# Attention and a mixture of experts on one core: weight differences for quarter products made earlier, and quarter products from group 1 on

## The chip, the cores and the metric

The kernel runs on one core of a Trainium2 chip. The time is device time in microseconds (us) of one execution. Three runs of the kernel before took 1044.04, 1045.3 and 1048.0 us; the median is 1045.3. The engines are TensorE (PE, with its weight loads PEld), VectorE (DVE), ScalarE (ACT) and GpSimd (POOL). SyncE (SP) issues DMAs, and so do POOL and ACT.

## The reference

Two steps. The first is attention for 8 batches and 8 heads of width 64: 32 global and 512 local tokens, where local tokens see the global ones and a band of 32 to each side. Its output is 4352 rows of 512 values, x, in batches of 544. The second is a mixture of 8 experts in which every row goes through every expert, weighted by a matrix P that eight normalisations over rows and columns make from the gate's logits:

```python
    logits = x @ w_gate
    logits = logits - logits.max()
    P = np.exp(logits)
    for _ in range(8):
        P /= P.sum(1, keepdims=True) + 1e-09
        P /= P.sum(0, keepdims=True) + 1e-09
        P *= N / E
    out = np.zeros((N, D), dtype=np.float32)
    for e in range(E):
        h = np.maximum(x @ w1[e], 0.0)
        ye = h @ w2[e]
        out += P[:, e:e + 1] * ye
```

Here D is 512, the hidden width F is 1024, E is 8, and the expert weights are w1 (512 x 1024) and w2 (1024 x 512).

## The kernel before

**Two parts.** The order of all instructions is written out by hand. The first part is a software pipeline over 32 slots, four to a batch; slot s works on a pair of heads of batch s // 4. It transposes q and k (`st_A`), makes scores (`st_B`), normalises them (`st_N`), transposes them (`st_D1`, `st_D2`) and multiplies by the values (`st_E`). Every second slot from 9 on carries a step for global queries (`st_G0`, `st_G1`), which ends in the slot after (`st_GN`, `st_G2`, `st_G3`). Between these steps, `f1` puts first-layer products of experts 0 to 3 on PE: relu(x w1), since P is positive and can be multiplied in later. `p_l1` makes eight of them, with ACT or DVE doing the relu (L471, L473), into a tile hT of 1 MB, and stores it to DRAM (hd). The first part's times repeat every 41.07 us, which is four slots.

**Buffers and queues of the first part.** The pool `hpool` has four buffers of 1 MB, tag hT. SP issues, in the order of the code, the loads of q and k (L122, four of 512 KB at the end of each slot 4b), the stores of hT and x, and moves of values. A queue waits in order: an instruction that waits holds all behind it. POOL casts q and k to fp16 (L131), issues the loads of values, and in slots 13, 17, 21 and 25 the conversion of w1 of experts 4 to 7 from fp32 to an fp16 copy in DRAM, w1d (L484).

**The second part** runs over units (m, e): group m is 512 rows (0 to 7, and a half group 8), and e runs in the order 4, 0, 5, 1, 6, 2, 7, 3. Units with an even number (experts 4 to 7) make the first layer here, from x scaled by P; those with an odd number (experts 0 to 3) load h from hd and scale it. The second layer is done for all units by seven half-size products in place of eight (`product`, L928), from sums and differences that DVE makes. While a pair of units has its second layer, the next even unit's first layer is made between those products, in one of two forms:

- the full form, `l1` (L818): 32 matmuls of 512 columns, weights from a tile w1s of 1 MB;
- the quarter form, class `Fast` (L836): seven products of quarter size for each half p of the hidden width, 56 matmuls of 256 columns in all. It needs weights w1q with four raw quarters and three sums and differences (7 x 2 x 256 values a partition, 896 KB for each half), differences of x on DVE (`sums_x`), and copies and additions of partial sums on ACT and DVE (L852, L854, L861, L868).

`WX = {6: 2, 7: 2}` says from which group an expert takes the quarter form: experts 6 and 7, from group 2 on, groups 0 to 7 being whole. `wseq` is the order in which weights go through two buffers (tag w1e); `load_w1` issues the loads on SP when a buffer's last user is done.

**The differences of the weights** are made in group 1. `wseq` holds, after each of the group's full units, an entry ("raw", p): four loads of 128 KB from w1d (L726), four DVE instructions in `prep_w1`, and a store of the 896 KB to w1c on POOL's queue (L741). From group 2 on, w1c is loaded with one DMA for each half (L729).

Of the kernel before, what the change touches and what calls it, by code (L numbers as in the profile page):

```python
# [9 lines left out]
FP16 = mybir.dt.float16  # L10
FP32 = mybir.dt.float32
AF = mybir.ActivationFunctionType
ALU = mybir.AluOpType
# [10 lines left out]
def kernel(  # L24
# [13 lines left out]
    nc = tc.nc  # L38
# [3 lines left out]
    D, E = moe_w_gate.shape  # L42
    F = moe_w1.shape[2]
    P = 128
# [6 lines left out]
    HP = H // 2  # L51
# [17 lines left out]
    hpool = ctx.enter_context(tc.tile_pool(name="hpool", bufs=4))  # L69
# [3 lines left out]
    NL = E // 2  # L73
    hd = [[ydram.tile([P, FT, n], FP16, name=f"hd{e}_{m}") for m, (_, n) in enumerate(groups)] for e in range(NL)]
    xd = [ydram.tile([P, DP, n], FP16, name=f"xd{m}") for m, (_, n) in enumerate(groups)]
    w1d = [ydram.tile([P, DP, F], FP16, name=f"w1d{e}") for e in range(NL, E)]
    pd = ydram.tile([E, NTOK], FP32, name="pd")
    WX = {6: 2, 7: 2}
    w1c = {e: [ydram.tile([P, 7, 2, 256], FP16, name=f"w1c{e}_{p}") for p in range(2)] for e in WX}
    psx = ExitStack()  # L80
    xpool = psx.enter_context(tc.tile_pool(name="xpool", bufs=1, side="right"))
# [10 lines left out]
    with tc.tile_pool(name="att_c", bufs=1) as att_c, \  # L92
# [121 lines left out]
        def run(steps):  # L214
            for f in steps:
                f()
# [6 lines left out]
        f0 = [att_in.tile([P, 4, NJ, Dh], FP32, tag="f32", name="f32", bufs=4) for t in range(2)]  # L223
        for i in range(2):
            for f, src, eng in zip(f0, (q_l, k_l), (nc.scalar, nc.sync)):
                eng.dma_start(out=f[:, 2 * i : 2 * i + 2].rearrange("p h s d -> p h (s d)"),
                              in_=src[0, 2 * i : 2 * i + 2].rearrange("h (p s) d -> p h (s d)", s=NJ))
# [9 lines left out]
        for a in range(2):  # L237
            r = slice(HB * a, HB * (a + 1))
# [15 lines left out]
        for so in range(NJ):  # L254
            for c0, n in ((W, P), (W + Sl, W // NJ)):
                nc.vector.tensor_copy(out=zsel[:, so, c0 : c0 + NJ * n].rearrange("p (x s) -> p x s", s=NJ)[:, :, so],
                                      in_=identity[:, 0:n])
# [143 lines left out]
        def st_G1(b, g):  # L401
            n0 = HP * b + 2 * g
            qg = qgbd[(2 * b + g) % 2]
            gc = slice(Sg * b, Sg * (b + 1))
            sg = ps_po.tile([P, 2 * 512], FP32, tag="po")
            for c0, c1, k0 in ((0, Sl - W, 2 * W), (Sl - W, Sl, W), (Sl, S, None)):
                for pr in range(2):
                    rhs = kgT[:, 2 * g + pr, gc] if k0 is None else kTe[(n0 + pr) % NK][:, k0 : k0 + c1 - c0]
                    nc.tensor.matmul(sg[:, c0:c1], qg[:, pr, :], rhs, start=(pr == 0), stop=(pr == 1))
            m2 = att_wk.tile([P, 4], FP32, tag="m2")  # L410
            nc.vector.reduce_max(out=m2[:, 0:1], in_=sg[:, 0:S], axis=AX.X)  # L411
            nc.vector.tensor_scalar(out=m2[:, 1:2], in0=m2[:, 0:1], scalar1=-scale, scalar2=None, op0=ALU.mult)
            Pg = att_wk.tile([P, S], FP16, tag="Pg")
            nc.scalar.activation(out=Pg, in_=sg[:, 0:S], func=AF.Exp, scale=scale, bias=m2[:, 1:2],
                                 accum_out=m2[:, 2:3])
            gs[(b, g)] = (Pg, m2)
# [60 lines left out]
        def load_w1e(e):  # L477
# [2 lines left out]
            wts[e] = pool.tile([P, DP, F], FP16, name="w1e", **kw)  # L480
            nc.gpsimd.dma_start(out=wts[e], in_=moe_w1[e].rearrange("(dko dki) f -> dki dko f", dki=P))

        def load_w1d(e):
            nc.gpsimd.dma_start(out=w1d[e - NL], in_=moe_w1[e].rearrange("(dko dki) f -> dki dko f", dki=P))  # L484

        fill = [(k % NL, k // NL) for k in range(NL * (B + 1))]
        n1 = 0
# [100 lines left out]
        for s in range(HP, NU + 1):  # L588
            slot = s
            b, hp = divmod(s, HP)  # L590
            g1 = s in gat
            g23 = s - 1 in gat
            if g1:
                gn = divmod(gat[s], 2)
            if g23:
                gp = divmod(gat[s - 1], 2)
            if s == HP:
                st_A(s + 1)
                st_B(s, 2)
                st_E(s - 1)  # L600
                st_N(s, 0, 6)
                st_N(s, 6, NHB)
                select_v(1, 0, (0, 1))
                st_B(s + 1, 0)
                select_v(1, 0, (2, 3))
                select_v(1, 1, (NJ - 1,))
                slot = s + 1
                va, vb = vab[1]
                nc.scalar.dma_start(out=vb[0:HB, 0 : NJ - 1], in_=va[HB:P, 0 : NJ - 1])
                nc.scalar.dma_start(out=vb[HB:P, 0 : NJ - 1], in_=va[0:HB, 1:NJ])  # L610
                cast_qk(1, 1, gq)
                gcast = [(cast_g(x[0], x[1]), x) for x in ((kgf, 1, kgT), (qgf, 0, qgT), (qgf, 1, qgT))]
                load_w1e(3)
            else:
                if HP + 1 < s <= 2 * HP:
                    st_B(s, 0)
                st_D1(s - 1)
                if g23:
                    st_GN(*gp)
            if g1 and s > HP + 1:  # L620
                st_G0(*gn)
            f1("aa")
            if 2 * HP < s < NU:
                st_B(s, 0)
            if s > HP:
                st_D2(s - 1)
            if g23:
                st_G2(*gp)
            if HP < s < NU:
                st_B(s, 1)  # L630
            if s > HP:
                f1("va")
            if HP < s < NU - 1:
                st_A(s + 1)
            if HP < s < NU:
                st_B(s, 2)
            if s > HP:
                f1("v")
                st_E(s - 1)
            if s == HP + 1:  # L640
                for t, (src, g, dst) in gcast:
                    transpose_g(t, g, dst)
                st_G0(*gn)
            if g23:
                st_G3(*gp)
            if s > HP:
                f1("va")
            if HP < s < NU:
                st_N(s, 0, 6)
                st_N(s, 6, NHB)  # L650
            if s > 2 * HP and not g1:
                f1("v")
            if s >= 5 and (s - 5) % HP == 0:
                logits(NJ * ((s - 5) // HP), NJ)
            if g1:
                st_G1(*gn)
            if s < NU and b + 1 < B:
                if hp == 0:
                    load_qk(b + 1, 0, (nc.sync, nc.sync))
                    load_qk(b + 1, 1, (nc.sync, nc.sync))  # L660
                elif hp == 1:
                    cast_qk(b + 1, 0, gq)
                    if b >= NL - 1:
                        load_w1d(b + 1)
                elif hp == 2:
                    vq = load_v(b + 1)
                    run(vq[:3])
                    cast_qk(b + 1, 1, gq)
                else:
                    run(vq[3:])  # L670
# [17 lines left out]
    def tt(out, in0, in1, op):  # L688
        nc.vector.tensor_tensor(out=out, in0=in0, in1=in1, op=op)  # L689
# [11 lines left out]
    units = [(m, e) for m in range(B + 1) for e in ORDER]  # L701
    NUN = len(units)
    w1s, pbs, xgs, xss, hs, ss, os_ = {}, {}, {}, {}, {}, {}, {}
# [2 lines left out]
        return i < NUN and units[i][0] < B and units[i][0] >= WX.get(units[i][1], B)  # L706

    wseq = [(i, p) for i in range(0, NUN, 2) for p in ((0, 1) if fast(i) else (None,))]
    for j, (e, p) in enumerate((e, p) for e in WX for p in range(2)):
        wseq.insert(wseq.index((E + 2 * j + 2, None)), (e, "raw", p))  # L710
    raw = {}
    wnext = 0

    def load_w1(used):
        nonlocal wnext
        while wnext < len(wseq) and (wnext < 2 or wseq[wnext - 2] in used):
            i, *p = wseq[wnext]
            if p[0] is None:
                w = w1s[i] = wpool.tile([P, DP, F], FP16, tag="w1e", name="w1s")
                nc.sync.dma_start(out=w, in_=w1d[units[i][1] - NL])  # L720
            else:
                w = wpool.tile([P, 7, 2, 256], FP16, tag="w1e", name="w1q")
                if p[0] == "raw":
                    for o, r, k in ((0, 0, 0), (1, 0, 1), (3, 1, 0), (2, 1, 1)):
                        f0 = 512 * r + 256 * p[1]
                        nc.sync.dma_start(out=w[:, o], in_=w1d[i - NL][:, 2 * k : 2 * k + 2, f0 : f0 + 256])  # L726
                    raw[wseq[wnext]] = w
                else:
                    nc.sync.dma_start(out=w, in_=w1c[units[i][1]][p[0]])  # L729
                    w1s[(i, p[0])] = w  # L730
            wnext += 1
            if wnext < 2:
                return

    def prep_w1():
        for k in list(raw):
            w = raw.pop(k)
            for o, a, b, op in ((5, 0, 3, ALU.subtract), (3, 3, 2, ALU.add), (4, 3, 0, ALU.subtract),
                                (6, 1, 4, ALU.subtract)):
                tt(w[:, o], w[:, a], w[:, b], op)  # L740
            nc.gpsimd.dma_start(out=w1c[k[0]][k[2]], in_=w)  # L741
            used.add(k)

    def load_pb(*us):
        us = [i for i in us if i < NUN]
# [314 lines left out]
    for fm in range(FT):  # L1060
        pool, tag = cyc[fm % 2]
# [4 lines left out]
    used = {(0, None)}  # L1066
# [6 lines left out]
    for i, (m, e) in enumerate(units):  # L1073
        if i == NUN - 1:
            last_pair(i)
        elif i % 2 == 0:
# [44 lines left out]
            else:  # L1121
                n = groups[m][1]
                h = hs[i + 1]
                s = ss[i + 1] = xsp.tile([P, HF, n], FP16, tag="xs", name="sl")
                tt(s, h[:, 0:HF, 0:n], h[:, HF:FT, 0:n], ALU.add)
            if m > 0:
                prep_w1()
            scale_x(i + 4)
            if m == 0:
                for e in {2: (2,), 4: (7,), 6: (3,)}.get(i, ()):  # L1130
# [83 lines left out]
```

## Time and profile before

| what | us |
|---|---|
| profiled execution | 1044.08 |
| its span, first to last instruction | 1042.2 |
| PE busy | 1015.2 |
| DVE busy | 868.7 |
| ACT busy | 513.0 |
| POOL busy | 139.7 |
| first-layer products of the first part (L468) | 255.9 |
| second-layer products (L928) | 199.9, 137.2 and 123.8 by the tiles they write and read |
| full first-layer products (L818) | 174.6 |
| DVE instructions on w1q, sixteen of 423 ns | 6.8 |

The span is the profiled execution without what lies ahead of the first and behind the last instruction. Busy times are unions, so they say how much of the span an engine works; they say nothing on who waits for whom. That is read from a timeline, where a line gives the start, the length, the instruction with its tiles and shapes, and in brackets the idle time of the engine just before it and what ended it. The first part lies between 0 and some 335 us, the normalisations of P until 377, and the second part from 395 on. The granted clock of PE was 0.995 of full speed over the span.

### The profile page before, as it was taken

To read this page: it belongs to the slowest core of one execution; us is meant where nothing else is said; L and a number is where in the kernel's file an instruction comes from. 1 tells how busy PE (TensorE), PEld (TensorE's weight loads), DVE (VectorE), ACT (ScalarE), POOL (GpSimd) and SP (SyncE) were. 2 spreads that over 40 slices of the span, in tenths; PEclk is the share of its full clock that TensorE was granted. 3 is DMA by queue.
4 is the path that set the end of the run, shared out by engine and by line. 5 is a ranking of instruction groups with operands and counts; after the bars stand their busy time and mean duration, and the time that the engine had idled before them with its cause. 6 is when DMAs were issued, how large, how long until landed. Compare 5 with 4: busy or idle time off the path is not lost.

```text
span 1042.2 us, 22693 instructions
## 1 busy us (share of the span) xinstructions
PE 1015.2 (97%) x9142; PEld 728.5 (70%) x9142; DVE 868.7 (83%) x1638; ACT 513.0 (49%) x1296; POOL 139.7 (13%) x227
## 2 busy tenths in 40 slices
PE   7899999999999999999999999999999999999998
PEld 4555555555555466777777877877877878878887
DVE  7687777777776786999889799889899898898895
ACT  7777878787876675223222333333333332332331
POOL 7442423414312102000000000000000000000000
PEclk9899999999999999999999999999999999999999
DMA  9887588988945999946756546454553555464470
GB/s 260 197 217 207 118 273 181 220 232 177 258 136 142 275 261 302 259 143 203 272 194 234 189 153 219 160 189 180 200 189 138 203 187 168 172 218 152 145 260 26
DMA packets 101960, 206.08 MB, mean 198 GB/s; under 512 B 33936, under 2 KB 68192, under 8 KB 90592
## 3 DMA queue, kind: packets, MB, share of 16 engines
q1 hardware_dynamic: 56064, 162.75, 45.1%
q0 software_dynamic: 43184, 32.26, 17.7%
q10 hardware_dynamic: 2608, 9.64, 2.4%
q8 instruction: 71, 1.16, 0.4%
q14 instruction: 33, 0.27, 0.1%
HBM read 168.64 MB, written 57.29 MB: 217 GB/s over the span
## 4 chain that ended last, share of the span: by engine, by line
PE 83%; ACT 8%; DVE 6%; issue 2%; DMA 1%; SPq 0%; POOL 0%; ACTq 0%; DVEq 0%
PE m L928 28%; PE ph L818 15%; PE ph L468 15%; PE pm L928 11%; PE pf L836 7%; ACT Pu L311 4%; DVE Pu L348 3%; PE ptw L359 1%; ACT hT L471 1%; ACT qbd L285 1%; PE pv L157 1%; PE pt L275 1%; DMA vraw<-in_v_l_dram 1%; PE po L380 1%; DVE m L411 1%
## 5 line engine op out<-in xcount | busy, mean ns | idle before, releaser
L468 PE MATMUL ph<-xT,w1e 128*128 128x512 f16 (+1 forms) x1152 | 255.9, 367 | 0.2
L928 PEld LDWEIGHTS <-h 128*128 128x128 f16 x2160 | 211.4, 98 | 36.6
L820 ACT ACTIVATE h<-ph 128x512 f16<-128x512 f32 (+1 forms) x192 | 107.5, 562 | 204.2 <-PE ph L818 202.2
L928 PE MATMUL m<-w2c,s 128*128 128x256 f16 x1620 | 199.9, 273 | 0.0
L928 PEld LDWEIGHTS <-s 128*128 128x128 f16 x1620 | 158.5, 98 | 30.5
L818 PE MATMUL ph<-xs,w1s 128*128 128x512 f16 (+1 forms) x768 | 174.6, 361 | 0.0
L468 PEld LDWEIGHTS <-w1e 128*128 128x128 f16 x1152 | 105.4, 98 | 96.1 <-issue 3.0
L689 DVE TENSOR_TENSOR h<-h,pb 128x2048 f16<-128x2048 f16 (+1 forms) x48 | 152.4, 3175 | 3.8 <-DMA h<-hd 3.7
L689 DVE TENSOR_TENSOR s<-h 128x1024 f16<-128x1024 f16 (+2 forms) x166 | 126.4, 803 | 24.3 <-PE m L928 16.9
L928 PE MATMUL m<-w2c,h 128*128 128x256 f16 x1080 | 137.2, 273 | 0.0
L471 ACT ACTIVATE hT<-ph 128x512 f16<-128x512 f32 (+1 forms) x192 | 104.4, 559 | 47.5 <-PE ph L468 45.2
L928 PE MATMUL pm<-w2c,h 128*128 128x256 f16 x1080 | 123.8, 273 | 0.0
L818 PEld LDWEIGHTS <-w1s 128*128 128x128 f16 x768 | 75.1, 98 | 52.6
L843 ACT ACTIVATE h<-pf 128x512 f16<-128x512 f32 x96 | 55.0, 596 | 84.1 <-PE pf L836 79.9
L311 ACT ACTIVATE Pu<-ms,mx 128x160 f16<-128x160 f32 x224 | 93.6, 420 | 5.2 <-DVE mx L308 2.7
L473 DVE TENSOR_SCALAR hT<-ph 128x512 f16<-128x512 f32 x96 | 66.1, 688 | 31.3 <-PE ph L468 30.5
L689 DVE TENSOR_TENSOR h<-h 128x1024 f16<-128x1024 f16 (+1 forms) x166 | 90.3, 586 | 0.0
L689 DVE TENSOR_TENSOR xs<-xg,pb 128x2048 f16<-128x2048 f16 (+1 forms) x36 | 78.1, 2169 | 12.8 <-DMA pb<-pd 12.8
L947 POOL DMA_DIRECT2D out_dram<-o x8 | 6.1, 758 | 533.3 <-DVE o L944 533.3
L308 DVE CUSTOM_DVE_ANT_0 ms<-sc,mask 128x160 f32<-128x160 f32 x224 | 59.9, 319 | 18.7 <-PE sc L303 18.2
L836 PEld LDWEIGHTS <-w1q 128*128 128x128 f16 x672 | 65.7, 98 | 7.7
L852 ACT COPY pf<-pf 128x512 f32<-128x512 f32 x24 | 13.7, 570 | 81.5 <-PE pf L836 81.5
(165 smaller groups left out, 1225.7 us busy)
## 6 DMA issues: line engine op xcount, KB each, us to landing
h<-hd SPq DMA_DIRECT2D x32, 1024.0 KB
hd<-hT SPq DMA_DIRECT2D x26, 1024.0 KB
w1s<-w1d SPq DMA_DIRECT2D x24, 1024.0 KB
w1q<-w1c SPq DMA_DIRECT2D x24, 896.0 KB
pb<-pd SPq DMA_DIRECT2D x64, 256.0 KB
w2c<-in_moe_w_dram POOLq DMA_DIRECT2D x16, 512.0 KB, 20.1
out_dram<-o POOLq DMA_DIRECT2D x8, 1024.0 KB, 4.6
f<-in_q_l_dram SPq DMA_DIRECT2D x15, 512.0 KB
```

Of the source, the lines that this page charges most:

```text
L308: nc.vector.tensor_tensor_reduce(out=ms[:, ii, :], in0=sc[:, SW * ii : SW * (ii + 1)], in1=mask[:, mi, :], scale=-scale, scalar=BIG, op0=A ...
L311: nc.scalar.activation(out=d["Pu"][:, i, :], in_=ms[:, ii, :], func=AF.Exp, scale=-1.0, bias=d["mx"][:, i : i + 1], accum_out=d["sm"][:, i ...
L348: nc.vector.tensor_tensor(out=d["Pu"][:, i0:i1, 0:KW], in0=d["Pu"][:, i0:i1, 0:KW], in1=d["rs"][:, i0:i1].unsqueeze(2).to_broadcast([P, i1 ...
L468: nc.tensor.matmul(ph[:, 0:n], wts[e][:, dk, P * fm : P * (fm + 1)], xT[m][:, dk, :], start=(dk == 0), stop=(dk == DP - 1))
L471: nc.scalar.activation(out=hT[:, fm, 0:n], in_=ph[:, 0:n], func=AF.Relu)
L473: nc.vector.tensor_scalar(out=hT[:, fm, 0:n], in0=ph[:, 0:n], scalar1=0.0, scalar2=None, op0=ALU.max)
L689: nc.vector.tensor_tensor(out=out, in0=in0, in1=in1, op=op)
L818: nc.tensor.matmul(ph[:, 0:n], w1s[i][:, dk, P * fm : P * (fm + 1)], xss[i][:, dk, 0:n], start=(dk == 0), stop=(dk == DP - 1))
L820: nc.scalar.activation(out=hs[i][:, fm, 0:n], in_=ph[:, 0:n], func=AF.Relu)
L836: nc.tensor.matmul(bank[:, 256 * c : 256 * (c + 1)], self.w[:, self.sta[q], k, P * c : P * (c + 1)], self.mov[q][:, k], start=(first and c ...
L843: nc.scalar.activation(out=self.h[:, k : k + 2, 256 * c : 256 * (c + 1)], in_=bank.rearrange("p (k t) -> p k t", k=2), func=AF.Relu)
L928: nc.tensor.matmul(pm[:, HD * t : HD * (t + 1)], lhs[0][:, k, lhs[1] + P * t : lhs[1] + P * (t + 1)], w[:, k, q - 1, :], start=(k == 0 and ...
```

## The change

`WX` becomes `{6: 1, 7: 1}`: two more units, those of experts 6 and 7 in group 1, take the quarter form. The differences of the weights are no longer made in group 1. `prep_w1`, the raw entries of `wseq` and the branch of `load_w1` for them are gone. Three new functions make them in the first part, one piece (expert 6 or 7, half p) after another, in a tile wq from `hpool`: `wq_load` issues the four loads on SP, `wq_sums` two of the four DVE instructions at a time, and `wq_store` the store, now on SP. They stand at the end of a slot's work, after `st_G1` and ahead of the loads of q and k. With HP = 4 the index is `divmod(s - 16, 2)`: piece 0 is loaded in slot 16, has its DVE instructions in slots 17 and 18 and its store in slot 18, where piece 1 is loaded, and so on; the last store, of piece 3, is in slot 24. Since experts 6 and 7 are needed first, the conversions of w1 to w1d are made in the order 6, 7, 4, 5.

```diff
-    WX = {6: 2, 7: 2}
+    WX = {6: 1, 7: 1}
...
+        W1D = list(WX) + [e for e in range(NL, E) if e not in WX]
+
         def load_w1d(e):
             nc.gpsimd.dma_start(out=w1d[e - NL], in_=moe_w1[e].rearrange("(dko dki) f -> dki dko f", dki=P))
+
+        wqs = [(e, p) for e in WX for p in range(2)]
+        wqt = {}
+
+        def wq_load(j):
+            if 0 <= j < len(wqs):
+                e, p = wqs[j]
+                w = wqt[j] = hpool.tile([P, 7, 2, 256], FP16, tag="hT", name="wq")
+                for o, r, k in ((0, 0, 0), (1, 0, 1), (3, 1, 0), (2, 1, 1)):
+                    f0 = 512 * r + 256 * p
+                    nc.sync.dma_start(out=w[:, o], in_=w1d[e - NL][:, 2 * k : 2 * k + 2, f0 : f0 + 256])
+
+        def wq_sums(j, part):
+            if 0 <= j < len(wqs):
+                w = wqt[j]
+                for o, a, b, op in ((5, 0, 3, ALU.subtract), (3, 3, 2, ALU.add), (4, 3, 0, ALU.subtract),
+                                    (6, 1, 4, ALU.subtract))[2 * part : 2 * part + 2]:
+                    nc.vector.tensor_tensor(out=w[:, o], in0=w[:, a], in1=w[:, b], op=op)
+
+        def wq_store(j):
+            if 0 <= j < len(wqs):
+                e, p = wqs[j]
+                nc.sync.dma_start(out=w1c[e][p], in_=wqt[j])
...
             if g1:
                 st_G1(*gn)
+            j, odd = divmod(s - 4 * HP, 2)
+            if odd:
+                wq_sums(j, 0)
+            else:
+                wq_sums(j - 1, 1)
+                wq_store(j - 1)
+                wq_load(j)
...
                     if b >= NL - 1:
-                        load_w1d(b + 1)
+                        load_w1d(W1D[b - NL + 1])
...
-    for j, (e, p) in enumerate((e, p) for e in WX for p in range(2)):
-        wseq.insert(wseq.index((E + 2 * j + 2, None)), (e, "raw", p))
-    raw = {}
...
-                if p[0] == "raw":
-                    for o, r, k in ((0, 0, 0), (1, 0, 1), (3, 1, 0), (2, 1, 1)):
-                        f0 = 512 * r + 256 * p[1]
-                        nc.sync.dma_start(out=w[:, o], in_=w1d[i - NL][:, 2 * k : 2 * k + 2, f0 : f0 + 256])
-                    raw[wseq[wnext]] = w
-                else:
-                    nc.sync.dma_start(out=w, in_=w1c[units[i][1]][p[0]])
-                    w1s[(i, p[0])] = w
+                nc.sync.dma_start(out=w, in_=w1c[units[i][1]][p[0]])
+                w1s[(i, p[0])] = w
...
-    def prep_w1():
-        for k in list(raw):
-            w = raw.pop(k)
-            for o, a, b, op in ((5, 0, 3, ALU.subtract), (3, 3, 2, ALU.add), (4, 3, 0, ALU.subtract),
-                                (6, 1, 4, ALU.subtract)):
-                tt(w[:, o], w[:, a], w[:, b], op)
-            nc.gpsimd.dma_start(out=w1c[k[0]][k[2]], in_=w)
-            used.add(k)
...
-            if m > 0:
-                prep_w1()
```

## The prediction

> **What bounds the kernel now.** I read the page's busy slices first, then the busy time of chosen stretches, then the timelines of TensorE (PE) and VectorE (DVE) in the two places that the change touches. The profiled execution took 1044.08 us; its span is 1042.2, so 1.9 us lie around it. The median of the three runs is 1045.3, 1.2 above it. Sums are made against 1044.08, and 1.2 is added at the end.
>
> ```profile
> PE   7899999999999999999999999999999999999998
> ...
> DVE  7687777777776786999889799889899898898895
> ```
>
> ```profile
> 186.00:227.00 41.00, 39.89 (x443) 22.51 (x442) 31.36 (x112) 33.51 (x106) 13.77 (x24) 1.00 0.88 218
> 490.50:567.03 76.53, 76.53 (x577) 56.36 (x576) 67.08 (x72) 21.50 (x36) 2.38 (x4) 1.00 0.65 235
> 567.03:641.98 74.95, 74.95 (x625) 61.05 (x624) 67.27 (x81) 25.39 (x44) 0.76 (x1) 1.00 0.52 183
> ```
>
> The first fence is the span in 40 slices, busy tenths. The second gives, after the stretch and its length, busy us of PE, its weight loads, DVE, ScalarE (ACT) and GpSimd (POOL), then granted clock, DMA share and GB/s. Its first row is four slots of the first part (18 to 21): PE 39.9 of 41.0, DVE 31.4. The other two are group 1 and group 2 of the second part, cut at the same product:
>
> ```profile
> 490.50 3.66 PE L928 MATMUL pm<-w2c,h 128*128 128x256 f16 x32
> ...
> 567.03 3.66 PE L928 MATMUL pm<-w2c,h 128*128 128x256 f16 x32
> ...
> 641.98 3.66 PE L928 MATMUL pm<-w2c,h 128*128 128x256 f16 x32
> ```
>
> In both, PE is busy for the whole stretch. So in the second part only PE's own work counts, and whatever DVE, the queues and POOL do in group 1 is hidden. In the first part the balance is fine-grained; its period of 41.07 us has 1.1 us of PE gaps. DVE there, at the end of a slot with an odd number (17, upper rows) and an even one (18, lower rows):
>
> ```profile
> 186.42 0.15 DVE L412 TENSOR_SCALAR m<-m 128x1 f32<-128x1 f32 x1
> 186.49 0.68 DVE L361 COPY pw<-ptw 128x1024 f16<-128x1024 f16 x1
> 187.51 0.16 DVE L420 RECIPROCAL m<-m 128x1 f32<-128x1 f32 x1 [0.33 <-ACT Pg L414]
> 187.71 0.54 DVE L421 TENSOR_SCALAR Pg<-Pg,m 128x544 f16<-128x544 f16 x1
> ...
> 196.36 0.68 DVE L473 TENSOR_SCALAR hT<-ph 128x512 f16<-128x512 f32 x1
> 196.96 0.68 DVE L361 COPY pw<-ptw 128x1024 f16<-128x1024 f16 x1
> 198.86 0.33 DVE L308 CUSTOM_DVE_ANT_0 ms<-sc,mask 128x160 f32<-128x160 f32 x1 [1.22 <-PE sc L303]
> ```
>
> ```profile
> 188.31 0.45 PE L428 MATMUL pt<-identity,Pg 128*128 128x128 f16 x5 [0.22 <-DVE Pg L421]
> ...
> 208.71 0.45 PE L428 MATMUL pt<-identity,Pg 128*128 128x128 f16 x5
> ```
>
> The bracket is idle time and what ended it. After an odd slot DVE has 0.33 us to spare ahead of L420, and PE's transposes of Pg wait for L421: 0.22 us after slot 17, and after slot 19 they start 0.06 us after L421's end (208.29 + 0.36 = 208.65). After an even slot DVE waits 1.22 us for PE anyway.
>
> **Part 1, two more units by quarter products.** Units 12 and 14 (group 1, experts 6 and 7) become what units 20 and 22 are. Group 2 has exactly that order of work, so the gain is the difference of the two stretches: 76.53 - 74.95 = 1.58 us. By matmuls: 32 of 512 columns at 0.867 us per four are 6.94; 56 of 256 columns at 0.436 per four are 6.10; twice 0.84 is 1.68, less a seam. I take 1.58. What comes along (more DVE sums, ACT copies, 1.75 MB of weights a unit in place of 1 MB) is hidden as in group 2, where DVE is busy 67.27 of 74.95 and PE has no gap; without that cover the price is the DVE work that two such units add, 67.27 - (67.08 - 6.84) = 7.0 us; how far PE would feel it is the fourth rival.
>
> **Part 2, the preparation leaves group 1.** Sixteen DVE subtractions, sixteen raw loads and four stores go. Four of the DVE ones:
>
> ```profile
> 486.53 1.80 DVE L689 TENSOR_TENSOR w1q<-w1q 128x512 f16<-128x512 f16 x4
> 488.24 2.28 DVE L689 TENSOR_TENSOR xs<-xg,pb 128x2048 f16<-128x2048 f16 x1
> ```
>
> (488.24 - 486.53) / 4 = 0.43 us each, 6.8 us in all. PE never waited for them, so they are worth 0 here, and so are the sixteen issues on SP and the four on POOL.
>
> **Part 3, the preparation enters slots 16 to 24.** By the code, piece j is loaded at the end of slot 16 + 2j, two of its four DVE instructions stand at the end of slot 17 + 2j, two at the end of slot 18 + 2j, then its store on SP. Slots 25 to 28 get nothing.
>
> *Even slots (18, 20, 22, 24).* Two instructions of 0.43 us, 0.86 together, stand between L473 and the pw copy. They move pw from 196.96 to 197.82, and 0.60 later DVE is at L308, at 198.42, still before the 198.86 at which PE lets it go. pw is read by PE after 202, by the same trace. Cost 0; without the 1.22 us of waiting it would be 0.86 each.
>
> *Odd slots (17, 19, 21, 23).* The pair stands between L412 and pw. pw starts at 186.49 + 0.86 = 187.35, L420 at 187.95 in place of 187.51: 0.44 late, and PE, which already waited for L421, waits 0.44 longer. What is queued behind it (scores for L308, ACT's exponentials, the next DVE pass) shifts by the same amount and not twice. After slots 19 and 23 there are 0.06 to spare: 0.38, say 0.40. Sum of the four: 0.44 + 0.40 + 0.44 + 0.40 = 1.68. Slot 17 also meets POOL:
>
> ```profile
> 186.08 1.03 POOL L131 CAST qs<-f 128x1024 f16<-128x1024 f32 x1
> 187.06 1.03 POOL L131 CAST ks<-f 128x1024 f16<-128x1024 f32 x1
> ```
>
> L421 takes 0.54 us beside such a cast and 0.36 without one (the row at 208.29). If each sum is stretched by those 0.18 us, slot 17 costs 0.36 more. In slot 21 the casts will start later (below) and miss the sums. So 2.04 us. Bounds: 0 (all of it falls into waits) and 16 x 0.43 = 6.8 (none does).
>
> *The queue of SP.* Each piece adds four loads (512 KB) and one store (896 KB), ahead of the q and k loads of the next batch at the ends of slots 16, 20 and 24. The store waits for DVE's last subtraction, at about the time at which SP reaches those loads anyway. Consecutive 512 KB loads land 1.45 us apart (by the semaphores, 223.3, 224.8, 226.3, 227.8 for those after slot 20), so 1408 KB put the four loads 4.0 us back. POOL's casts at 227.15 then wait some 3 us; POOL has 7.38 us free before its next normalisation (196.13 in the period shown), which covers it (without it, some 3 us in slot 21). The weight copies that POOL issues behind the casts change their order (experts 6, 7, 4, 5 in slots 13, 17, 21, 25); each is 10 us in landing (8.1 to 11.9), piece 0 reads its copy 28 us after the issue at 146.96, and expert 4's is first read at 385.5: 0. The moves of value rows on SP (L170 to L166) end near 217 in the period shown, and PE needs them after 222; 5 us cover what the added traffic delays them. Two landings are tight. The third piece's loads queue behind the hT store of 217.51, which landed at 223.77, and the 896 KB store (2.5 us): about 228, with the 1.2 us that slots 17 and 19 have cost by then 229.2, against a need at 227.56 + 1.2 = 228.8. And the program's waits show that, while two pieces are alive, the hT tiles take turns in two buffers in place of four: a tile's first write needs the store before the last one landed. The store issued at 229.07 landed at 235.21, 5.6 us after the last of the loads ahead; 5.2 us later it lands at 240.4, against a need at 239.46 + 1.7 = 241.1. For these I take 0.5, between 0 and 2 each.
>
> **Sum.** -1.58 + 2.04 + 0.5 = +0.96 us: 1045.0 by the profiled execution, 1046.3 by the median.
>
> **Rivals.**
> *The sums hide altogether.* DVE is idle 24% of this stage, and each slot's waits add up to over 2 us. Against it: the 0.33 and 0.06 us above. Then only the gain is left: 1044.08 - 1.58 = 1042.5, median 1043.7.
> *Two buffers are too few (slower).* Place: the first hT write of a tile, from slot 19 to 22, on ACT or DVE, with PE's filler products behind it. It decides once a 1 MB store takes longer than the filling of a tile (10.5 us). For it: the store issued at 261.23, behind four loads, took 10.8 us. Against it: the others took 3.9 to 7.0. Four tiles at 1.5 us late are 6: 1044.08 - 1.58 + 2.04 + 6 = 1050.5, median 1051.8.
> *Casts and sums shut each other out.* For it: L421's 0.54, which ends 0.16 us after the cast does. Against it: in slot 21 the casts come late. Then in slots 17 and 21 the first sum waits for the cast's end (187.1), the second cast runs to 188.55, the second sum to 188.98, and L421 ends 1.85 us late in place of 0.80 and 0.44: +2.46: 1047.5, median 1048.7.
> The Trainium skill ("SBUF — State Buffer", "SBUF: two separate sides") states it as a rule: a Vector instruction with two SBUF inputs and a GpSimd one that reads SBUF exclude each other for a whole instruction. By that rule the time would be this rival's; the row of L421 agrees with it, but that one has a single tensor input.
> *No gain.* Group 1's DVE can't carry the quarter products after all and PE waits as much as it saves: so the 1.58 is not there: 1046.6, median 1047.8. Group 2's gapless PE speaks against it.
>
> **How the numbers follow.** Forecast 0.49, hidden 0.20, two buffers 0.14, shut out 0.13, no gain 0.04. Half a per cent, about what a measurement can tell here from no change, is 5.2 us: 1040.1 to 1050.5. Faster than that none of the cases gives (PE has no gaps to win); 0.04 is left for what I don't see. Slower: most of two buffers, and little of shut out and the forecast's tail: 0.16. The forecast's own range is 1044.5 to 1048.5. For 8 in 10 the low end takes in the hidden case with the run spread, 1042.8, and the high end half of two buffers, 1051.5.
>
> **What would show it.** Group 1 between the same products in 74.95 us, PE without a gap: part 1 and 2. Slots 17 to 24 longer than 82.1 us by 2 to 2.5, in pieces of about 0.4 ahead of L428, and none ahead of L308: part 3. L428's wait after slot 17 at 1.0 against 0.66 after slot 21: the casts. DVE idle ahead of the sums with a load as releaser, or ACT ahead of hT with hd: the landings. Wrong if group 1 keeps 76.5 us, if the slots don't lengthen, or if the time goes to a place outside both.

## The result, and the profile after

Seventeen runs of the changed kernel have a median of 1049.75 us (1047.36 to 1051.54), seventeen of the kernel before 1044.58 (1042.56 to 1048.0). The ratio is 1.0047, with an interval of 1.0038 to 1.0056; by it the change makes the kernel 4.9 us slower. The profiled execution took 1050.04 us with a span of 1048.2, which is 6.0 more than before.

Busy time by stretch in the changed kernel; the columns are those of the rows shown for the kernel before. The first row is slots 16 to 31 of the first part, cut at the start of the transposes of `st_D1`, the second is group 1 between the same two products as before:

```profile
164.83:335.81 170.98, 161.31 (x1765) 90.36 (x1761) 131.74 (x460) 133.09 (x422) 48.75 (x83) 0.99 0.85 220
497.68:572.63 74.95, 74.95 (x626) 61.06 (x625) 68.25 (x82) 25.40 (x44) 0.76 (x1) 1.00 0.51 183
```

The same sixteen slots of the kernel before:

```profile
164.78:328.62 163.84, 159.54 (x1765) 89.73 (x1761) 125.06 (x444) 132.84 (x422) 47.71 (x83) 1.00 0.77 195
```

Group 1 takes 74.95 us in place of 76.53, so the 1.58 us of gain are there. The slots take 170.98 in place of 163.84: 7.14 us are lost. Together that is +5.56 of the span's 6.0; the other 0.4 lie behind group 1. The loss is read from PE's transposes of Pg, which wait for L421. In the changed kernel's timeline, those after slots 17, 19, 21 and 23:

```profile
189.75 0.45 PE L428 MATMUL pt<-identity,Pg 128*128 128x128 f16 x5 [1.61 <-DVE Pg L421]
212.97 0.45 PE L428 MATMUL pt<-identity,Pg 128*128 128x128 f16 x5 [2.78 <-DVE Pg L421]
235.52 0.45 PE L428 MATMUL pt<-identity,Pg 128*128 128x128 f16 x5 [0.43 <-DVE Pg L421]
256.99 0.45 PE L428 MATMUL pt<-identity,Pg 128*128 128x128 f16 x5 [1.02 <-DVE Pg L421]
```

Before, the four waited 0.22, 0, 0.22 and 0. The extra waits are 1.39 + 2.78 + 0.21 + 1.02 = 5.40 us. Two of them have causes of their own. DVE after slot 17, and POOL at the same time:

```profile
186.48 0.15 DVE L412 TENSOR_SCALAR m<-m 128x1 f32<-128x1 f32 x1
186.59 2.03 DVE L504 TENSOR_TENSOR wq<-wq 128x512 f16<-128x512 f16 x2
188.55 0.68 DVE L361 COPY pw<-ptw 128x1024 f16<-128x1024 f16 x1
```

```profile
186.14 1.03 POOL L131 CAST qs<-f 128x1024 f16<-128x1024 f32 x1
187.12 1.24 POOL L131 CAST ks<-f 128x1024 f16<-128x1024 f32 x1
```

The pair of subtractions takes 2.03 us beside the casts (0.86 and 1.14), and the second cast 1.24 in place of 1.03. DVE after slot 19:

```profile
208.44 0.15 DVE L412 TENSOR_SCALAR m<-m 128x1 f32<-128x1 f32 x1
210.96 0.89 DVE L504 TENSOR_TENSOR wq<-wq 128x512 f16<-128x512 f16 x2 [2.37 <-DMA wq<-w1d]
...
212.55 0.36 DVE L421 TENSOR_SCALAR Pg<-Pg,m 128x544 f16<-128x544 f16 x1
```

Here no cast runs, the pair takes 0.89, but the second piece's loads have not landed and hold DVE, and all that is queued behind, for 2.37 us. In slot 23 the same wait is 0.34 and 0.30, for the fourth piece. Of the 1.74 us that are missing between 5.40 and 7.14, 1.72 are in slot 20, and the column of the granted clock (the third from the right) tells of them:

```profile
209.00:213.00 4.00, 1.22 (x13) 0.67 (x12) 1.97 (x6) 1.47 (x4) 0.72 (x2) 1.00 1.20 313
213.00:215.00 2.00, 2.00 (x16) 1.12 (x17) 1.47 (x12) 1.75 (x8) 0.00 (x0) 0.71 0.50 32
215.00:217.00 2.00, 2.00 (x9) 0.88 (x8) 0.69 (x1) 1.87 (x8) 0.00 (x0) 0.50 0.69 131
217.00:219.00 2.00, 2.00 (x46) 1.34 (x44) 1.45 (x6) 1.12 (x3) 0.00 (x0) 0.94 0.54 164
```

PE idles for 2.78 us, and about 0.9 us after it is back its clock falls to half, for 3.4 us. PE is then busy all the time, at half speed. Slot 20 takes 15.01 us in place of 10.51: 2.78 of waiting and 1.72 of slow clock.

### The profile page after: what moved, and what is told of

Same layout as the page of the kernel before. It is cut to its first block, busy times and chain, and to the rows that moved or that the text cites. A ratio compares the mean times of both kernels' runs of the same rounds, so it can differ in the third digit from the quotient of the medians.

```text
span 1048.2 us, 22843 instructions
## 1 busy us (share of the span) xinstructions
PE 1015.7 (97%) x9190; PEld 733.8 (70%) x9190; DVE 877.7 (84%) x1664; ACT 517.0 (49%) x1304; POOL 138.6 (13%) x223
## 3 DMA queue, kind: packets, MB, share of 16 engines
q8 instruction: 72, 1.18, 0.4%
## 4 chain that ended last, share of the span: by engine, by line
PE 82%; DVE 7%; ACT 6%; DMA 2%; issue 2%; SPq 1%; POOL 0%; ACTq 0%; DVEq 0%
PE m L942 28%; PE ph L468 14%; PE ph L832 13%; PE pm L942 11%; PE pf L850 8%; DVE Pu L348 3%; ACT Pu L311 3%; DMA wq<-w1d 2%; PE pv L157 1%; PE ptw L359 1%; PE pt L275 1%; ACT hT L471 1%; DMA vraw<-in_v_l_dram 1%; PE po L380 1%; ACT qbd L285 1%
## 5 line engine op out<-in xcount | busy, mean ns | idle before, releaser
L834 ACT ACTIVATE h<-ph 128x512 f16<-128x512 f32 (+1 forms) x176 | 98.0, 559 | 170.4 <-PE ph L832 165.4
L832 PE MATMUL ph<-xs,w1s 128*128 128x512 f16 (+1 forms) x704 | 158.9, 360 | 0.0
L857 ACT ACTIVATE h<-pf 128x512 f16<-128x512 f32 x112 | 64.1, 596 | 98.2 <-PE pf L850 93.5
L832 PEld LDWEIGHTS <-w1s 128*128 128x128 f16 x704 | 68.9, 98 | 47.6
L850 PEld LDWEIGHTS <-w1q 128*128 128x128 f16 x784 | 76.7, 98 | 8.9
L308 DVE CUSTOM_DVE_ANT_0 ms<-sc,mask 128x160 f32<-128x160 f32 x224 | 60.0, 320 | 15.9 <-PE sc L303 15.3
L866 ACT COPY pf<-pf 128x512 f32<-128x512 f32 x28 | 16.0, 570 | 95.0 <-PE pf L850 95.0
```

What stands on the lines that cost most here:

```text
L308: nc.vector.tensor_tensor_reduce(out=ms[:, ii, :], in0=sc[:, SW * ii : SW * (ii + 1)], in1=mask[:, mi, :], scale=-scale, scalar=BIG, op0=A ...
L832: nc.tensor.matmul(ph[:, 0:n], w1s[i][:, dk, P * fm : P * (fm + 1)], xss[i][:, dk, 0:n], start=(dk == 0), stop=(dk == DP - 1))
L834: nc.scalar.activation(out=hs[i][:, fm, 0:n], in_=ph[:, 0:n], func=AF.Relu)
L850: nc.tensor.matmul(bank[:, 256 * c : 256 * (c + 1)], self.w[:, self.sta[q], k, P * c : P * (c + 1)], self.mov[q][:, k], start=(first and c ...
L857: nc.scalar.activation(out=self.h[:, k : k + 2, 256 * c : 256 * (c + 1)], in_=bank.rearrange("p (k t) -> p k t", k=2), func=AF.Relu)
```

## The experiments

All eight are variants of the changed kernel and were timed beside the kernel before, which had a median of 1044.4 in the first four and 1044.1 in the last four.

### Loads one slot earlier

```diff
-            j, odd = divmod(s - 4 * HP, 2)
-            if odd:
-                wq_sums(j, 0)
-            else:
-                wq_sums(j - 1, 1)
-                wq_store(j - 1)
-                wq_load(j)
+            for j in range(4):
+                if s == 17 + 2 * j:
+                    wq_sums(j, 0)
+                if s == 18 + 2 * j:
+                    wq_sums(j, 1)
+                    wq_store(j)
+            for j in range(4):
+                if s == 15 + 2 * j:
+                    wq_load(j)
```

> The changed kernel with each piece's loads issued one slot earlier (end of slot 15 + 2j in place of 16 + 2j); DVE's instructions and the stores stay where they are. Landing theory (the loss is DVE held by loads that have not landed, ahead of the transposes L428, and the PE clock that fell after the longest of these waits): DVE waits for no load, the granted clock stays 1.0 in slots 19 to 21 (1.7 us back), and L428's extra waits are about 1.4 us after slot 17 and after slot 21 (both then meet POOL's casts), 0.4 after slots 19 and 23: 3.6 - 1.58 = +2.0 us on the kernel before, 1046.6. Rival, the volume theory (5.6 MB more through the queue of SP and two hT buffers in place of four cost the time, wherever the loads stand): nothing changes, +5.1 us, 1049.7, and the time shows at ACT or DVE ahead of hT.

Measured: 1045.42 us, ratio 1.0015 (1.0006 to 1.0024). The sixteen slots, in the profile of this run:

```profile
164.28:330.63 166.35, 159.64 (x1765) 89.72 (x1761) 131.77 (x460) 132.86 (x422) 48.76 (x83) 1.00 0.86 227
```

2.51 us are lost in place of 7.14, the clock stays at 1.00, and DVE waits for no load. PE waits 1.61 after slot 17 as before the move (1.39 more than in the kernel before), and 0.34 after slots 19 and 23. After slot 21 it is 0.57, not 1.61, since the casts there are late; so this part of the expectation was too high. The traffic is the same, so the volume theory falls. The loads not only have a slot more here: they no longer stand behind the store of the piece before in SP's queue, nor beside POOL's value loads (by the semaphores they landed in 3.3 to 8.1 us). The run doesn't tell these apart.

### All pairs in even slots

The three conditions become these:

```diff
-                if s == 17 + 2 * j:
+                if s == 16 + 4 * j:
                     wq_sums(j, 0)
-                if s == 18 + 2 * j:
+                if s == 18 + 4 * j:
...
-                if s == 15 + 2 * j:
+                if s == (15, 18, 22, 26)[j]:
```

> The same sixteen DVE instructions, two at the end of each even slot from 16 to 30, none in odd slots; loads at the ends of slots 15, 18, 22 and 26, two slots ahead of their first use. Position theory (only the place ahead of L421 costs; after an even slot DVE waits 1.22 us for PE anyway): PE's gaps in slots 16 to 30 are those of before, the first part keeps its length within 0.3 us, and the gain of the two units is all that is left: -1.6 us, 1043.0. Rival (DVE's added 6.8 us and the added traffic cost by their amount): +2 to +5 us, 1046.6 to 1049.7.

Measured: 1042.51 us, ratio 0.9984 (0.9975 to 0.9992), which is faster than the kernel before. The sixteen slots, and DVE at the end of slot 20, in the profile of this run:

```profile
164.07:327.91 163.84, 159.54 (x1765) 89.75 (x1761) 131.18 (x460) 132.86 (x422) 49.35 (x83) 1.00 0.90 230
```

```profile
216.06 0.68 DVE L473 TENSOR_SCALAR hT<-ph 128x512 f16<-128x512 f32 x1
216.66 0.87 DVE L504 TENSOR_TENSOR wq<-wq 128x512 f16<-128x512 f16 x2
217.45 0.68 DVE L361 COPY pw<-ptw 128x1024 f16<-128x1024 f16 x1
218.56 0.33 DVE L308 CUSTOM_DVE_ANT_0 ms<-sc,mask 128x160 f32<-128x160 f32 x1 [0.42 <-PE sc L303]
```

163.84 us, to the hundredth what the kernel before takes, with 6.1 us more of DVE work in it (131.18 against 125.06). The pair eats into DVE's wait ahead of L308, 0.42 in place of 1.22, and nothing moves: the position theory holds, and its rival falls. The loads at the end of slot 18 are as slow here as in the changed kernel: by the semaphores, issued at 197.57 to 200.41, the last one landed at 209.16. They simply have two slots. So the lateness was not made smaller, it was covered.

### Odd slots with casts, odd slots without

The first has the pairs of a piece at the ends of slots 17 + 4j and 18 + 4j, the second at 19 + 4j and 20 + 4j, each with its loads two slots ahead.

```diff
-                if s == 17 + 2 * j:
+                if s == 17 + 4 * j:
                     wq_sums(j, 0)
-                if s == 18 + 2 * j:
+                if s == 18 + 4 * j:
...
-                if s == 15 + 2 * j:
+                if s == 15 + 4 * j:
```

> One pair of a piece at the ends of slots 17, 21, 25 and 29, where POOL casts q and k at the same time, the other pair one slot later; loads two slots ahead of the first pair. Cast theory (the two engines shut each other out): each pair in an odd slot takes about 2.0 us in place of 0.87, and PE waits 1.4 us longer for L421 in each of the four: 5.6 - 1.58 = +4.0 us, 1048.6. Rival (an odd slot costs 0.4 us wherever it is, and what slot 17 showed beyond that was particular to it): +0.0 us, 1044.6, the same as with slots 19, 23, 27 and 31.

> As the run with slots 17, 21, 25 and 29, but with slots 19, 23, 27 and 31, where POOL casts nothing; the second pair of the last piece then stands at the end of slot 32. Cast theory: each pair takes 0.87 us, PE waits 0.4 us longer after each of the four slots, and up to 0.9 us may show at slot 32: 1.6 - 1.58 = 0.0 us, 1044.6 to 1045.5, some 4 us less than with the casts. Rival (no difference between odd slots): the same time as with slots 17, 21, 25 and 29.

Measured: 1047.04 us with casts, ratio 1.0026 (1.0016 to 1.0037), and 1045.56 without, 1.0011 (1.0002 to 1.0019). In the run with casts, DVE's pairs in slots 21 and 29, and POOL in slot 21:

```profile
228.59 2.03 DVE L504 TENSOR_TENSOR wq<-wq 128x512 f16<-128x512 f16 x2
```

```profile
313.52 0.88 DVE L504 TENSOR_TENSOR wq<-wq 128x512 f16<-128x512 f16 x2
```

```profile
228.14 1.03 POOL L131 CAST qs<-f 128x1024 f16<-128x1024 f32 x1
229.11 1.23 POOL L131 CAST ks<-f 128x1024 f16<-128x1024 f32 x1
```

Slots 17, 21 and 25 have the casts, and there the pair takes 2.03 and PE waits 1.61 ahead of L428. Slot 29 has none (there is no batch to cast for), and there the pair takes 0.88 and PE's wait is 0.46 in place of 0.05. Three times 1.39 and 0.41 are 4.58; the sixteen slots took 168.42, which is 4.58 above 163.84. The expectation was 1.6 us high, 1.0 of it because it counted four slots with casts, and there are three.

Without casts the pairs took 0.88 or 0.89, PE waited 0.34 to 0.37 after slots 19, 23 and 27 and 0.78 in place of 0.22 after slot 21 (a late cast, below), and the sixteen slots lost 1.78. Behind them PE lost 0.97 more: 0.42 after slot 31, and 0.55 at the last pair, in slot 32. Less the gain of 1.58 that is +1.17, and the median is 1.18 above that of the kernel before. So the cast theory holds for the length of a pair (2.03 against 0.88) and for the wait behind it; that the two runs lie 1.5 us apart and not 4 is for the fourth cast that isn't there, the late one that is, and slot 32.

The run without casts shows the same exclusion on an instruction that both kernels have. In its slot 21 the second cast is late, and L421 meets its start:

```profile
228.96 1.10 DVE L421 TENSOR_SCALAR Pg<-Pg,m 128x544 f16<-128x544 f16 x1
```

```profile
228.86 1.04 POOL L131 CAST ks<-f 128x1024 f16<-128x1024 f32 x1 [0.45 <-DMA f<-in_k_l_dram]
```

L421 took 0.36 alone, 0.54 in the kernel before and 1.10 here; it ends 0.16 us after the cast in both cases (188.25 against 188.09, 230.06 against 229.90). Its end follows the end of the cast and not its own start, so it was not slowed by a share, it waited for the cast.

### The differences in even slots, group 1 as before

```diff
-    WX = {6: 1, 7: 1}
+    WX = {6: 2, 7: 2}
```

> The even-slot kernel with WX = {6: 2, 7: 2}: the differences are made in the first part's even slots, but group 1 keeps the full form. If the even slots cost nothing and the gain is the two units alone: the kernel before, 1044.4, and 1.6 us above the even-slot kernel; group 1 between the same products in 76.53 us in place of 74.95. Rival (part of the even-slot kernel's gain comes from group 1 being rid of the sixteen DVE instructions, the raw loads and their place in the two weight buffers): it keeps part of the gain, 1043 to 1043.5.

Measured, with the pairs in even slots: 1043.93 us, ratio 0.9998 (0.999 to 1.0007). Group 1 in this run's timeline runs from the first to the second of these products:

```profile
491.52 3.66 PE L944 MATMUL pm<-w2c,h 128*128 128x256 f16 x32
...
568.05 3.66 PE L944 MATMUL pm<-w2c,h 128*128 128x256 f16 x32
```

76.53 us, as in the kernel before, without the sixteen subtractions and their loads. So the removal is worth nothing, and the gain of the even-slot kernel is that of the two units.

### Casts moved one slot later

```diff
                 elif hp == 1:
-                    cast_qk(b + 1, 0, gq)
...
                     run(vq[:3])
+                    cast_qk(b + 1, 0, gq)
                     cast_qk(b + 1, 1, gq)
```

Once with the pairs in slots 17, 21, 25 and 29, once with the pairs in even slots.

> The kernel with pairs in slots 17, 21, 25 and 29, with POOL's first pair of casts of every batch moved one slot later, behind the value loads of the slot after. Cast theory: the pairs take 0.87 us in place of 2.00, L421 takes 0.36 us, PE waits about 0.4 us longer after each of the four slots in place of 1.4 (three times): some 3 us less than with the casts beside them, and the 0.2 us that PE waits after each such slot of the kernel before goes too: 1043.5 to 1044.5. Rival (another thing in these slots, such as the gate product or the weight conversion, makes the pairs slow): 1047, as with the casts in place.

> The even-slot kernel with POOL's first pair of casts moved one slot later. Cast theory: L421 no longer meets a cast and takes 0.36 us in place of 0.54 in slots 9, 13, 17, 21 and 25, where PE waited 0.22 us: up to 0.2 us a batch, 1 us in all, 1041.5 against 1042.5. Rival (the casts come late for the global step's copies on POOL, which queue behind them, and PE waits there): no gain or up to 2 us lost.

Measured: 1050.94 us, ratio 1.0064 (1.0052 to 1.0077), and 1048.96, 1.0044 (1.0032 to 1.0057). Both are far above what either theory expected. DVE in slot 21 of the first, then PE in its slots 19 and 22:

```profile
232.90 0.89 DVE L504 TENSOR_TENSOR wq<-wq 128x512 f16<-128x512 f16 x2
```

```profile
206.03 0.40 PE L275 MATMUL pt<-identity,ks 128*128 128x128 f16 x4 [1.20 <-POOL ks L131]
...
234.91 0.45 PE L428 MATMUL pt<-identity,Pg 128*128 128x128 f16 x5 [0.46 <-DVE Pg L421]
```

The part on the casts held: without them the pair takes 0.89, and PE's wait falls from 1.61 to 0.46 in the three slots that had casts; in the fourth it was 0.46 with no cast already. In the kernel with even slots it falls from 0.23 to 0.04. But POOL now casts k only behind its value loads, and `st_A` needs it in the very next slot: PE waits for the cast six times, 6.3 us in all in each of the two. A wait of 0.2 us a batch was given away for one of 1.05.

### PE's own work put into the wait

```diff
+            if s == 20:
+                f1("va")
             if g23:
                 st_G2(*gp)
             if HP < s < NU:
                 st_B(s, 1)
-            if s > HP:
+            if s > HP and s != 20:
                 f1("va")
```

> The changed kernel with one move of PE's work: in slot 20 the two first-layer products that stand behind the second scores are put ahead of the transposes L428, so that PE has 1.7 us of its own work to do while it waits for L421. Clock theory (the wait of 2.8 us after slot 19 makes PE's clock fall to half for 3.4 us, which costs 1.7 us by itself): the wait shrinks to about 1 us, the granted clock stays at 1.0, and the time falls by the 1.7 us of work and by another 1.7 us: 1049.7 - 3.4 = 1046.3. Rival (the clock's fall has another cause, or costs nothing because PE waits anyway): 1.7 us less at most, 1048.0, with the clock still at 0.5 in slot 20.

Measured: 1048.29 us, ratio 1.004 (1.0026 to 1.0054). PE after slot 19, ACT, and slot 20, in this run:

```profile
212.58 0.45 PE L428 MATMUL pt<-identity,Pg 128*128 128x128 f16 x5 [1.01 <-DVE Pg L421]
...
214.51 0.38 PE L275 MATMUL pt<-identity,ks 128*128 128x128 f16 x4 [1.24 <-ACT pg L369]
```

```profile
212.86 0.43 ACT L311 ACTIVATE Pu<-ms,mx 128x160 f16<-128x160 f32 x1 [2.74 <-DVE mx L308]
```

```profile
206.94:219.91 12.97, 10.62 (x119) 5.77 (x114) 8.76 (x32) 8.73 (x29) 2.23 (x3) 1.00 0.87 178
```

DVE still waits 2.33 us for the loads. PE idles 1.01 us ahead of L428 in place of 2.78, but 1.24 more ahead of its next transposes, which wait for ACT's copy L369; ACT had waited for DVE's L308, which stands behind L421. So the idle time is 2.25 us, in two parts, and the clock stays at 1.00. Slot 20 takes 12.97 us in place of 15.01: it gains the 1.72 of the clock and 0.32 of the 1.7 us of work that was moved, since the rest of the late chain, over DVE and ACT, is waited for a little later. In whole runs the gain is not clear of the noise: the ratio of the changed kernel, 1.0047, lies inside this run's interval, and the time is near the rival's 1048.0, not 1046.3. The clock theory is right on the clock, in one profiled execution, and wrong on what the moved work would bring.

## Why the prediction was right or wrong

The time lies in the range for 8 in 10, 1042.8 to 1051.5, and the ratio, 1.0047, just within half a per cent of no change, with an interval that reaches past it. The forecast itself, 1 us above the kernel before, was 4 us too low; its own range ended at 1048.5. That the time still lies in the wide range is luck in part: the upper end was set by half of the rival of two buffers, and that rival did not come.

- *Two more units, 1.58.* Right: group 1 takes 74.95 us, with PE without a gap, and the run that keeps WX at 2 loses just that.
- *Preparation out of group 1, 0.* Right, by the same run (ratio 0.9998).
- *Even slots, 0.* Right; DVE's wait of 1.22 covers the pair, 0.42 is left.
- *Odd slots without a cast, 0.40 to 0.44.* Right: 0.34 to 0.41 measured. In slot 21 it was 0.21, since the late casts that the text foresaw (POOL waited 2.17 and 0.46 us for them) also left L421 alone.
- *Slot 17 beside the casts, 0.80.* Wrong in size: 1.39. The 0.18 by which L421 was stretched was read as a slowing of so much for each instruction. It was the rest of a wait for the cast's end. The third rival had this mechanism and put 1.85 on it, in two slots; it happened in one. The rule that the Trainium skill states ("SBUF — State Buffer", "SBUF: two separate sides"), that a Vector instruction with two SBUF inputs and a GpSimd one that reads SBUF exclude each other for a whole instruction, holds here, by pairs of 2.03 us beside casts and 0.88 without.
- *Landings, 0.5.* This is the term that was mis-sized most: 3.0 us of DVE waiting (2.37 + 0.34 + 0.30). The prediction called the third piece's loads tight, and those landed in time, at 233.08 for a pair that starts at 233.51; the second and the fourth piece's didn't. They are issued at the ends of slots 18 and 22, where POOL issues value loads, and in SP's queue behind the store of the piece before. By the semaphores the second piece's last load landed at 211.17 after its issue at 202.71, each of the four in 7.7 to 9.9 us, where the same loads took 2.2 to 2.8 in group 1 of the kernel before; and the value loads took 9.4 in place of 4.5. The prediction counted SP's own transfers ahead of a load, at 1.45 us per 512 KB, and left out the value loads. (The four landings that it lists for that rate, 223.3 to 227.8, are those of each load's first part; the last parts landed at 225.2 to 229.6, 1.45 apart as well.) In slot 20, which has no value loads, its count comes out: the store of 896 KB landed 2.15 us after the 1 MB store ahead of it, and the last load 1.36 after that; in slot 18 the same two steps took 4.48 and 5.07. So the value loads are the likely cause, but this is argued from landing times; no run took them alone away.
- *The clock.* Not in the prediction at all: 1.72 us, in the profiled execution. In the kernel before, PE waits no longer than 0.7 us at a time from 34 us on, and its clock is whole from 43 us until the last 2. It had fallen once, near the start (the 8 in the second of the 40 slices of the clock, below, where 9 is 90% or more), and the prediction passed over that: a wait was priced at its own length only.

```profile
PEclk9899999999999999999999999999999999999999
```

- *Two buffers for hT.* The rival did not come: the stores of 1 MB from slot 17 to slot 24 took 3.9 to 9.3 us, less than the filling of a tile, and the profile shows no wait of ACT or DVE for one.

## What to carry to other kernels

Work that is free in one place of a balanced pipeline costs in the next one: the same sixteen instructions cost nothing ahead of a wait of 1.2 us, and 0.4 us a pair ahead of a wait of 0.3. Put them where the trace shows their engine waiting longer than they take, and away from another engine's instructions that they exclude, here the casts. Don't take the landing time of their loads from a quiet stage: here it was 7.7 to 9.9 us against 2.2 to 2.8. Done so, the change brings what its arithmetic promised: 1042.51 us, ratio 0.9984 (0.9975 to 0.9992).

## What the runs showed of the hardware

An idle time of PE of 2.78 us was enough to halve its granted clock for 3.41 us, starting 0.9 us after PE was busy again. Waits of 1.61 us left it whole, and so did 1.01 and 1.24 shortly after each other in the run with the filled wait. This is one profiled execution; in those of the other nine kernels PE waits no longer than 1.61 us at a time from slot 16 on, and the clock is whole there until the last 4 us. The mean clock of the changed kernel's seventeen runs lies between 0.993 and 0.998, so it need not have fallen in each of them. The Trainium skill ("TensorE: Matmul & The Clock Gate", "HAM oscillation — how this bites in real kernels") puts the bound at gaps of more than about 3.4 us; here the shorter gap sufficed, and the measurement decides. What else counts isn't settled: near the start of the kernel before, the clock fell to half for 10 us with no single wait above 1.9 us ahead of it.

A Vector instruction with one tensor input (L421, fp16 in and out, 0.36 us alone) also waits out a GpSimd cast, to 0.16 us after its end (0.54 us in the kernel before, 1.10 in the run without casts beside the pairs), and a cast waits for a subtraction: 1.24 us in place of 1.03.
